# A decode step with attention and a gated FFN: later FFN weights, fp32 transposes, a PV bank shared by four pairs, and half of the last K moved to TensorE

## The chip, the cores and the metric

The kernel runs on one core of one Trainium2 chip. The metric is the device time of one execution in microseconds (us). A core has five engines that run side by side: TensorE (PE in the profile, PEld for its weight loads), VectorE (DVE), ScalarE (ACT), GpSimd (POOL) and SyncE (SP). Sixteen DMA engines bring data from memory. "Span" is the length of the profiled execution; the time that is measured from outside is about 2 us longer.

## The reference, cut to what matters

```python
# B=2, D=512, H=32 heads, Sk=8192 cached positions, Dh=128, F=1376, all bf16
q  = layernorm(x) @ wq
s  = q . k_cache * Dh**-0.5          # one query per head: a matrix-vector product
o  = softmax(s) @ v_cache
h  = x + o @ wo
g  = relu(layernorm(h) @ W_gate) * (layernorm(h) @ W_up)
out = h + g @ W_down
```

K and V are 268 MB of the 281 MB that are read, and each byte is used once.

## The kernel before

Heads go through the kernel in 32 pairs (p = 0 to 31). A pair's K is one tile of 128 partitions with 128 vectors of 128 numbers each (4 MB), and so is its V. Of the 128 columns of K, 96 are scored on VectorE, in two halves of 48: a product with q, four halving additions, a reduction. The other 32 are scored by TensorE, in four groups of eight: transpose, eviction by ACT, product with q.

```python
for p in range(NP):
    for c in range(NCH):                      # VectorE: two halves of 48 columns
        dve.wait(t_k[p])
        t_dm = prod = k_t[half c] * q         # then 4 halving additions
        t_s  = scores = reduce(prod)
        if c == 0:
            for g in range(NG):               # TensorE: 4 groups of 8 columns
                for k in range(GT):
                    i = nc.tensor.transpose(Tp[n % 2][:, k*128:(k+1)*128], k_t[:, j, :], ident[:])
                t_ev[n] = act.run(nc.scalar.activation(out=kT[n % 3][:], in_=Tp[n % 2][:], func=ACT.Copy))
                if g >= 1: score_group(p, g - 1)
            score_group(p, NG - 1)
            exp(p, 0, ...)                    # ACT, with the row sums
            if p == NP - 1: pv(p - 1)
            if p >= 1:      collect(p - 1)
        act.wait(t_s)
        exp(p, 1 + c, ...)                    # ACT works in this order
    load of K(p + 2); pv(p); load of V(p + 2) # ... cut
    # at p == 30: W_up, W_gate, then V(31) in four parts, then W_down
```

PV multiplies with the exps as weights and V as the moving operand, 512 columns wide, so four partial results stand beside each other in the bank. `collect` copies them to SBUF and adds the four diagonal blocks with four fp32 matmuls against a selection matrix, once per pair. After the last pair come the sum of the exps, PV of pair 31 column by column, the output projection, d_b (the centred input of the FFN), and the FFN.

The softmax here doesn't subtract the row's maximum and nothing guards it: scores larger than these inputs give would overflow.

## Time and profile before

| | before |
|---|---|
| time, median of 4 runs | 672.92 us (672.45 to 672.94) |
| span, instructions | 670.7 us, 8986 |
| read from memory | 281 MB |
| K of pair 30 landed | 623.98 us |
| d_b done | 662.26 us |

From the page: first line, then the slices of a fortieth of the span (share of the TensorE clock in tenths, DMA busy in tenths, GB/s) and two rows of the DMA queues (packets, MB, share of 16 engines).

```profile
span 670.7 us, 8986 instructions
PEclk9999999665565555655556656655566555565555
DMA  9999999999999999999999999999999999999994
GB/s 375 434 436 357 434 435 430 427 431 429 434 433 427 428 433 433 425 436 425 434 433 427 431 436 424 431 432 431 437 426 425 434 432 433 426 430 431 428 409 146
q1 hardware_dynamic: 15872, 281.06, 98.4%
q8 instruction: 30, 0.49, 0.3%
```

The DMA engines are busy from start to end, at about 430 GB/s. The row PEclk shows TensorE's granted clock near full for the first seven slices and at 5 to 6 tenths from then on. The first slices mean little: the trace holds no clock record before 117.8 us, and the row shows full where there is none (20 matmuls of PV take 2.31 us at 85 us and 2.31 us again at 124 us, where 0.50 is recorded). Every engine waits for the loads in mid-run, directly or in turn; the longest such row of the wait view (us in total, times, longest):

```profile
DVE prod L407 <- DMA slot<-in_A_k_cache_dram: 126.9, 30, 16.4
```

The row "q8 instruction" is easy to pass over, and I passed over it: 30 packets that carry the program itself to the engines, on the same DMA engines.

The end of the chain of work that ended last (start us, us, what):

```profile
637.07 22.22 DMA slot<-in_A_v_cache_dram
659.34 1.45 PE O L354 x48
...
662.10 0.17 DVE d_b L503
...
666.97 0.22 DVE o_c L567
```

The tail waits for the last part of V, queued behind the weights of the FFN, until 659.3. The timeline shows what else is close to the limit: VectorE's last scores, and PV of pair 30 on TensorE.

```profile
645.00 3.58 PE L361 MATMUL O<-slot,e 128*8 128x512 bf16 x32
655.05 0.55 DVE L424 TENSOR_REDUCE scores<-prod 128x48 f32<-128x384 bf16 x1
```

### The profile page before, as it was taken

The numbers are of one execution on the slowest core, as the hardware profiler recorded it, in microseconds if no ns is written. First come the engines' busy times: TensorE is split into PE (matmuls) and PEld (weight loads), VectorE is DVE, ScalarE is ACT, GpSimd is POOL, SyncE is SP. The second block draws the span as 40 slices with busy tenths as digits, with TensorE's granted clock in tenths as the row PEclk, the third lists the DMA queues.
The fourth block names the chain that finished last, engine by engine and source line by source line (L and its number), as shares of the span: only waits on it lengthen the run. The fifth ranks groups of instructions, "written<-read, shape, count | busy, mean of one in ns | idle before, by whom it ended". The sixth has DMA issues, their size and how long they took to land.

```text
span 670.7 us, 8986 instructions
## 1 busy us (share of the span) xinstructions
PE 352.0 (52%) x3868; PEld 234.1 (35%) x3868; DVE 494.4 (74%) x430; ACT 220.1 (33%) x554; POOL 2.5 (0%) x16
## 2 busy tenths in 40 slices
PE   2553355455545455554554655454556565455655
PEld 2431333233433223343322433232234443223435
DVE  1774477788768678877777887677786977678792
ACT  0631322233432234344222333322333342233340
POOL 1000000000000000000000000000000000000000
PEclk9999999665565555655556656655566555565555
DMA  9999999999999999999999999999999999999994
GB/s 375 434 436 357 434 435 430 427 431 429 434 433 427 428 433 433 425 436 425 434 433 427 431 436 424 431 432 431 437 426 425 434 432 433 426 430 431 428 409 146
DMA packets 15915, 281.63 MB, mean 420 GB/s; under 512 B 1442, under 2 KB 6916, under 8 KB 7044
## 3 DMA queue, kind: packets, MB, share of 16 engines
q1 hardware_dynamic: 15872, 281.06, 98.4%
q8 instruction: 30, 0.49, 0.3%
q14 instruction: 9, 0.07, 0.0%
q10 hardware_dynamic: 4, 0.00, 0.0%
HBM read 281.05 MB, written 0.00 MB: 419 GB/s over the span
## 4 chain that ended last, share of the span: by engine, by line
DMA 72%; DVE 22%; PE 3%; ACT 2%; issue 1%; SPq 0%; DVEq 0%
DMA slot<-in_A_k_cache_dram 68%; DVE prod L407 14%; DVE tb L415 4%; DMA slot<-in_A_v_cache_dram 3%; DVE prod L415 2%; ACT kT L440 1%; DVE scores L424 1%; PE T L434 1%; PE Ob L378 1%; ACT e L282 0%; PE S L274 0%; ACT os_sb L372 0%; PE Ob L295 0%; PE S L518 0%; PE O L560 0%
## 5 line engine op out<-in xcount | busy, mean ns | idle before, releaser
L407 DVE TENSOR_TENSOR prod<-slot,q_b 128x6144 bf16<-128x6144 bf16 x64 | 214.9, 3358 | 128.2 <-DMA slot<-in_A_k_cache_dram 126.9
L361 PE MATMUL O<-slot,e 128*8 128x512 bf16 x992 | 116.3, 621 | 143.4 <-ACT e L282 127.8
L440 ACT ACTIVATE kT<-T 128x1024 bf16<-128x1024 bf16 x128 | 126.2, 1021 | 160.2 <-PE T L434 159.4
L434 PE MATMUL T<-ident,slot 128*128 128x128 bf16 x1024 | 122.0, 305 | 65.3 <-DMA slot<-in_A_k_cache_dram 65.3
L415 DVE TENSOR_TENSOR tb<-prod 128x3072 bf16<-128x3072 bf16 (+1 forms) x128 | 148.2, 1158 | 4.4
L434 PEld LDWEIGHTS T<-ident,slot 128*128 128x128 bf16 x1024 | 99.3, 140 | 92.3 <-DMA slot<-in_A_k_cache_dram 90.6
L282 ACT ACTIVATE e<-scores 64x48 bf16<-64x48 f32 x128 | 32.8, 256 | 239.2 <-DVE scores L424 237.6
L361 PEld LDWEIGHTS O<-slot,e 128*8 128x8 bf16 x992 | 24.0, 106 | 209.6 <-ACT e L282 155.6
L415 DVE TENSOR_TENSOR prod<-tb 128x1536 bf16<-128x1536 bf16 (+1 forms) x128 | 84.2, 658 | 4.4
L378 PE MATMUL Ob<-sel,os_sb 128*128 128x2 f32 x248 | 57.5, 354 | 47.7 <-ACT os_sb L372 47.7
L378 PEld LDWEIGHTS Ob<-sel,os_sb 128*128 128x128 f32 x248 | 54.9, 327 | 51.2 <-ACT os_sb L372 51.2
L274 PE MATMUL S<-qT,kT 128*128 128x2 bf16 x1024 | 48.2, 168 | 39.2 <-ACT kT L440 38.1
L274 PEld LDWEIGHTS S<-qT,kT 128*128 128x128 bf16 x1024 | 40.7, 106 | 57.5 <-ACT kT L440 57.5
L424 DVE TENSOR_REDUCE scores<-prod 128x48 f32<-128x384 bf16 x64 | 35.4, 553 | 2.2
L282 ACT ACTIVATION_READ_ACCUMULATOR e<-scores 64x1 f32 x128 | 23.6, 185 | 0.0
L372 ACT ACTIVATE os_sb<-O 128x512 f32<-128x512 f32 x31 | 18.5, 597 | 3.4 <-PE O L361 2.7
L282 ACT ACTIVATE e<-S 64x32 bf16<-64x32 f32 x64 | 12.9, 202 | 15.0 <-PE S L274 14.2
L282 ACT ACTIVATION_READ_ACCUMULATOR e<-S 64x1 f32 x64 | 12.8, 201 | 0.7
L251 ACT ACTIVATE q_b<-O 128x512 bf16<-128x512 f32 x8 | 4.3, 595 | 15.8 <-PE O L246 15.8
L222 DVE CAST qT<-W 128x64 bf16<-128x64 f32 x1 | 0.2, 224 | 12.2 <-PE W L217 12.2
L217 PE MATMUL W<-xlT,X 128*128 128x2 bf16 x128 | 3.6, 166 | 8.8 <-DMA X<-in_A_wq_dram 8.8
L217 PEld LDWEIGHTS W<-xlT,X 128*128 128x128 bf16 x128 | 3.5, 104 | 8.8 <-DMA X<-in_A_wq_dram 8.8
(67 smaller groups left out, 58.8 us busy)
## 6 DMA issues: line engine op xcount, KB each, us to landing
slot<-in_A_k_cache_dram SPq DMA_DIRECT2D x32, 4096.0 KB, 27.7
slot<-in_A_v_cache_dram SPq DMA_DIRECT2D x31, 4096.0 KB, 31.3
X<-in_A_wq_dram SPq DMA_DIRECT2D x1, 4096.0 KB, 12.5
X<-in_A_wo_dram SPq DMA_DIRECT2D x1, 4096.0 KB, 48.7
slot<-in_A_v_cache_dram SPq DMA_DIRECT2D x1, 1536.0 KB, 19.8
slot<-in_B_W_up_dram SPq DMA_DIRECT2D x1, 1376.0 KB, 10.0
slot<-in_B_W_gate_dram SPq DMA_DIRECT2D x1, 1376.0 KB, 14.6
slot<-in_A_v_cache_dram SPq DMA_DIRECT2D x1, 1280.0 KB, 22.2
```

The costliest lines, as they stand in the source:

```text
L217: i = nc.tensor.matmul(Wp[:, h * B:(h + 1) * B], lhsT=wq[:, c, h * Dh:(h + 1) * Dh], rhs=lT[:, c * B:(c + 1) * B], start=(c == 0), stop=(c ...
L251: t_cp[m] = act.run(nc.scalar.activation(out=q_b[:, m * 512:(m + 1) * 512], in_=Op[m % 2][:], func=ACT.Copy))
L274: i = nc.tensor.matmul(Sp[p % 2][:, 2 * jj:2 * jj + 2], lhsT=kT[n % 3][:, k * 128:(k + 1) * 128], rhs=qT[:, 2 * p:2 * p + 2], start=True, ...
L282: t = act.run(nc.scalar.activation(out=e_t[p % 2][q, j0:j0 + nj, a], in_=src(q, a), func=ACT.Exp, scale=inv_sqrt_dh, accum_out=zs[q, 2 * p ...
L361: i = nc.tensor.matmul(o[g:g + 2 * VJ, :], lhsT=e_t[p % 2][:, j:j + VJ, :].rearrange("p j a -> p (j a)"), rhs=v_t[:, j:j + VJ, :].rearrang ...
L372: t_os[p] = act.run(nc.scalar.activation(out=os_sb[:], in_=Op[p % 2][:], func=ACT.Copy))
L378: i = nc.tensor.matmul(Ob[:, 2 * p:2 * p + 2], lhsT=os_sb[:, jj * Dh:(jj + 1) * Dh], rhs=sel[:, 2 * jj:2 * jj + 2], start=(jj == 0), stop= ...
L407: t_dm = dve.run(nc.vector.tensor_tensor(out=prod[:], in0=k_t[:, c * JC:(c + 1) * JC, :], in1=qv, op=ALU.mult))
L415: dve.run(nc.vector.tensor_tensor(out=o, in0=cur[:, :, 0:half], in1=cur[:, :, half:w], op=ALU.add))
L424: t_s = dve.run(nc.vector.tensor_reduce(out=sc[:], in_=cur, axis=AX.X, op=ALU.add))
L434: i = nc.tensor.transpose(Tp[n % 2][:, k * 128:(k + 1) * 128], k_t[:, j, :], ident[:])
L440: t_ev[n] = act.run(nc.scalar.activation(out=kT[n % 3][:], in_=Tp[n % 2][:], func=ACT.Copy))
```

## The change

Four things, aimed at the tail and at the load of TensorE and ACT:

1. **Order of loads.** V of the last pair is queued right after V of pair 30, in two parts; W_up, W_gate and W_down come last, each with its own semaphore.
2. **fp32 transposes.** Two neighbouring bf16 columns of K are transposed as one fp32 word, so half as many transposes are needed; the scores then use every second column and a q that is laid out to match.
3. **Shared PV bank.** Four pairs accumulate into one bank, each in eight of 32 rows (the others are multiplied with zeros), and `collect` runs once for four pairs.
4. **Half of the last K on TensorE.** Pair 31 gives 64 columns to TensorE (eight groups) and 32 to each half on VectorE.

The diff, cut to its core:

```diff
+                def split(p):
+                    ng = 2 * NG if p == NP - 1 else NG
+                    jc = (J - ng * GT) // NCH
+                    return ng, jc, [(NCH * jc, J)] + [(c * jc, (c + 1) * jc) for c in range(NCH)]
 # transposes
-                                for k in range(GT):
-                                    j = NCH * JC + g * GT + k
-                                    i = nc.tensor.transpose(
-                                        Tp[n % 2][:, k * 128:(k + 1) * 128], k_t[:, j, :], ident[:])
+                                for k in range(GT // 2):
+                                    j = parts[0][0] + g * GT + 2 * k
+                                    i = nc.tensor.transpose(
+                                        Tp[n % 2][:, k * 128:(k + 1) * 128],
+                                        k_t[:, j:j + 2, :].rearrange("p j d -> p (j d)").bitcast(F32), ident_f[:])
 # scores
+                    kv_ = kT[n % 2][:].rearrange("p (k n r) -> p k r n", n=128, r=2)
+                        for r in range(2):
+                            i = nc.tensor.matmul(
+                                Sp[p % 2][:, 2 * jj:2 * jj + 4], lhsT=kv_[:, k, r, :],
+                                rhs=q2[:, p, r, :], start=(r == 0), stop=(r == 1))
 # PV and collect
-                                o[g:g + 2 * VJ, :], lhsT=e_t[p % 2][:, j:j + VJ, :].rearrange("p j a -> p (j a)"),
+                                Op[gr % 2][c:c + 32, :], lhsT=e_t[qd][:, j // VJ, :],
-                            if p >= 1:
-                                collect(p - 1)
+                            if p >= 1 and (p % PG == 0 or p == NP - 1):
+                                collect((p - 1) // PG)
 # loads at p == 30 (... cut)
+                        sp.wait(t_pv[p - 1])
+                        for k, (j0, j1) in enumerate(((J // 2, J), (0, J // 2))):   # V(31)
                         sp.wait(*t_kfree[p])
                         for k, w in enumerate((B_W_up, B_W_gate)):
-                        load_v(p + 1, vparts)
+                        for k, (r0, r1) in enumerate(WD_PARTS):                      # W_down in two parts
```

## The prediction

> **What bounds the kernel.** The page's slice table shows DMA at 9 tenths in 39 of 40 slices, at about 430 GB/s; 281 MB at that rate take 654 of the 670.7 us span. The Trainium skill ("DMA: Bandwidth & Descriptors", section "Where 436 GB/s comes from") gives 435 GB/s as the fabric's ceiling; the trace's plateau of 425 to 437 agrees. In mid-run every engine waits for K (wait view: VectorE 127 us, PE 65 us). A pair takes 19.4 us of DMA; VectorE needs 15.5, PE and ACT less. So what the change saves there (per pair, three quarters of the selection matmuls' 1.87 us and of os_sb's 0.6 us) is off the critical path: worth about 0. The same bytes are loaded, so only the tail can move.
>
> **The tail before** (timeline, chain of waits): the last K lands at 633.7, VectorE ends its scores at 655.6, the last V part lands at 659.3, its PV ends at 660.8, d_b at 662.3, the end is at 670.7. DMA traffic ends at about 663 (one-microsecond windows). The 8.4 us from d_b on are bound by compute, not loads.
>
> **What the change does there.**
> - V of the last pair is queued 13 us earlier, ahead of 4.1 MB of FFN weights: estimated (9.5 us at 430 GB/s before 663), it lands at 653 to 654. This wait goes.
> - VectorE's last scores: 32 columns a half, not 48: 15.5 -> about 10.5 us, done at 650, not 655.6.
> - TensorE and ACT get 8 groups, not 4. ACT can start evicting only at 640.2, behind the exps of the pair before. Two groups took 2.36 us, so they end at about 649.8 (before 645.1). Then in order: PV of pair 30 3.6 us, os_sb 0.65, selection matmuls 1.9, two sums of 0.6, first half of PV 31 1.9, o_proj 1.2, second half 1.9, scale and last o_proj 0.8, d_b 0.8: d_b at about 663.7. A serial chain on PE replaces the waits for V and VectorE.
> - fp32 transposes: half as many, each with a slower weight load. The trace's fp32 selection matmuls come every 234 ns (two passes each), bf16 transposes every 128. The Trainium skill ("TensorE: Matmul & The Clock Gate", "Terms") says transpose mode makes fp32 4x faster; no run shows it yet. My estimate: one pass, 4 per group in about 0.95 us against 1.01, so the group rate stays. If a group costs 0.5 us, the tail gains 1 us; if 1.8 us, it loses about 5.
> - FFN after d_b: unchanged 8.4 us; the last weights land at about 663, needed at 665 or later.
>
> Sum: 0 in the middle, +1.4 us in the tail, less something for a cheaper transpose: nearly no change, 673.3 us, 8 in 10 between 670.3 and 675.8. Chances: faster by over 2% 0.015, within 2% 0.96, slower by over 2% 0.025.
>
> **What would show it.** Right: slices still at 9 and 430 GB/s; the chain ends not in a V load but in PE and ACT work of the last pair; V lands before 655, waited for by nobody; d_b at 662 to 665; 528 fp32 transposes at about 240 ns each. Wrong: FFN weights on the chain's end, or d_b before 661 (a tail shorter by 2 to 3 us: transposes or PE faster than assumed).
>
> **What would make it wrong.** fp32 transposes in several passes at over 450 ns; strided score weights loading slowly; a DMA plateau other than 430 GB/s; the last FFN load, in 1 KB packets, draining so unevenly that it sets the end.

## The result, and the profile after

The changed kernel took 669.17 us (median of 4 runs: 669.11, 671.62, 668.97, 669.24), before 672.92. The ratio is 0.9954 (95% interval 0.9931 to 0.9978); ratios are the mean time of one kernel's fast runs over that of the other's of the same rounds, so not quite the ratio of the medians. It is a gain of half a per cent, and below the range that I had given (670.3 to 675.8). Note the 671.62: it matters below.

The same parts of the page, after:

```profile
span 667.3 us, 7705 instructions
DMA  9999999999999999999999999999999999999995
q1 hardware_dynamic: 15600, 281.06, 98.8%
q8 instruction: 25, 0.41, 0.3%
```

DMA is as busy as before, with the same 281.06 MB of data, but 1281 instructions fewer, fetched in 25 packets instead of 30. The end of the chain has no load left in it (some of its longer pieces):

```profile
643.72 1.03 ACT kT L465
...
648.03 1.87 PE O L375 x32
...
652.33 1.59 PE O L392 x64
...
658.02 0.17 DVE d_b L536
...
663.35 0.22 DVE o_c L602
```

That is the chain that I had forecast (evictions, PV of pair 30, selection, PV of pair 31, d_b), but d_b is done at 658.2, not at 663.7. Two things differ. First, the chain starts earlier. K of pair 30 landed at 622.61 instead of 623.98; these are VectorE's first products of that pair in the timelines, before and after (in brackets the idle time ahead of it and what ended it):

```profile
623.98 3.36 DVE L407 TENSOR_TENSOR prod<-slot,q_b 128x6144 bf16<-128x6144 bf16 x1 [3.97 <-DMA slot<-in_A_k_cache_dram]
```

```profile
622.61 3.36 DVE L433 TENSOR_TENSOR prod<-slot,q_b 128x6144 bf16<-128x6144 bf16 x1 [3.94 <-DMA slot<-in_A_k_cache_dram]
```

Second, TensorE speeds up within the chain. These are two groups of transposes and PV of pair 30 in the timeline after, then the one-microsecond windows around the change (busy time and instructions of each engine, granted TensorE clock, DMA share, GB/s):

```profile
642.59 1.09 PE L458 MATMUL T<-ident_f,slot 128*128 128x128 f32 x4
...
645.01 0.64 PE L458 MATMUL T<-ident_f,slot 128*128 128x128 f32 x4
...
647.96 1.91 PE L375 MATMUL O<-slot,e 128*32 128x512 bf16 x32
```

```profile
core 0: us, PE busy (x) PEld busy (x) DVE busy (x) ACT busy (x) POOL busy (x), PEclk, DMA share, GB/s
642.00:643.00 1.00, 1.00 (x12) 0.66 (x11) 0.93 (x3) 0.88 (x2) 0.00 (x0) 0.50 1.00 426
643.00:644.00 1.00, 1.00 (x15) 0.79 (x14) 0.93 (x3) 0.72 (x2) 0.00 (x0) 0.63 1.08 459
644.00:645.00 1.00, 0.57 (x12) 0.34 (x11) 1.00 (x1) 1.00 (x2) 0.00 (x0) 1.00 0.96 410
...
653.00:654.00 1.00, 1.00 (x45) 1.00 (x42) 0.00 (x0) 0.00 (x0) 0.00 (x0) 0.99 1.00 396
654.00:655.00 1.00, 1.00 (x36) 1.00 (x35) 0.00 (x0) 0.00 (x0) 0.00 (x0) 0.50 1.07 407
```

The granted clock rises from 0.50 to 1.00 at about 643.7 and falls back at about 654. Meanwhile a group of transposes takes 0.64 us instead of 1.09, and PV 1.91 us where the kernel before needed 3.58.

So there were two theories to test, each with rivals:

- **Fetch.** The K stream runs ahead because fewer instruction packets ride on the DMA engines. Rivals: chance in the order of packets; less traffic of the engines on the buffers.
- **Clock.** The tail is shorter than forecast because the clock rises in it. Rivals: the fp32 transposes themselves; the order of loads alone; the split of K alone.

### The profile page after: what moved, and what is told of

Its sections match the earlier page's. It is cut to its first block, busy times and chain, and to the rows that moved or that the text cites. A ratio compares the mean times of both kernels' runs of the same rounds, so it can differ in the third digit from the quotient of the medians.

```text
span 667.3 us, 7705 instructions
## 1 busy us (share of the span) xinstructions
PE 320.9 (48%) x3224; PEld 198.0 (30%) x3224; DVE 490.5 (74%) x433; ACT 211.4 (32%) x535; POOL 5.8 (1%) x17
## 3 DMA queue, kind: packets, MB, share of 16 engines
q1 hardware_dynamic: 15600, 281.06, 98.8%
## 4 chain that ended last, share of the span: by engine, by line
DMA 68%; DVE 22%; PE 5%; ACT 3%; issue 1%; SPq 0%; DVEq 0%; ACTq 0%
DMA slot<-in_A_k_cache_dram 68%; DVE prod L433 14%; DVE tb L441 5%; DVE prod L441 3%; PE T L458 2%; ACT kT L465 2%; DVE scores L448 1%; PE Ob L408 1%; PE S L294 1%; ACT e L304 1%; PE O L392 0%; ACT os_sb L402 0%; PE O L375 0%; PE S L551 0%; PE Ob L319 0%
## 5 line engine op out<-in xcount | busy, mean ns | idle before, releaser
L433 DVE TENSOR_TENSOR prod<-slot,q_b 128x6144 bf16<-128x6144 bf16 (+1 forms) x64 | 212.8, 3324 | 127.1 <-DMA slot<-in_A_k_cache_dram 124.3
L375 PE MATMUL O<-slot,e 128*32 128x512 bf16 x992 | 115.8, 619 | 209.4 <-ACT e L304 133.0
L458 PE MATMUL T<-ident_f,slot 128*128 128x128 f32 x528 | 134.7, 422 | 65.4 <-DMA slot<-in_A_k_cache_dram 65.3
L441 DVE TENSOR_TENSOR tb<-prod 128x3072 bf16<-128x3072 bf16 (+2 forms) x128 | 146.9, 1147 | 4.4
L458 PEld LDWEIGHTS T<-ident_f,slot 128*128 128x128 f32 x528 | 97.2, 217 | 91.9 <-DMA slot<-in_A_k_cache_dram 90.2
L441 DVE TENSOR_TENSOR prod<-tb 128x1536 bf16<-128x1536 bf16 (+2 forms) x128 | 83.6, 653 | 4.4
L294 PE MATMUL S<-q,kT 128*128 128x4 bf16 x1056 | 50.1, 169 | 39.2 <-ACT kT L465 39.0
L294 PEld LDWEIGHTS S<-q,kT 128*128 128x128 bf16 x1056 | 43.7, 108 | 69.2 <-ACT kT L465 67.2
L448 DVE TENSOR_REDUCE scores<-prod 128x48 f32<-128x384 bf16 (+1 forms) x64 | 35.1, 549 | 2.3
L408 PEld LDWEIGHTS Ob<-sel,os_sb 128*128 128x128 f32 x64 | 13.4, 311 | 12.7 <-ACT os_sb L402 12.7
```

The source lines that it names most:

```text
L294: i = nc.tensor.matmul(Sp[p % 2][:, 2 * jj:2 * jj + 4], lhsT=kv_[:, k, r, :], rhs=q2[:, p, r, :], start=(r == 0), stop=(r == 1))
L375: i = nc.tensor.matmul(Op[gr % 2][c:c + 32, :], lhsT=e_t[qd][:, j // VJ, :], rhs=v_t[:, j:j + VJ, :].rearrange("p j d -> p (j d)"), start= ...
L408: i = nc.tensor.matmul(Ob[:, 2 * p0:2 * p0 + 2 * PG], lhsT=os_sb[:, jj * Dh:(jj + 1) * Dh], rhs=sel[:, 2 * PG * jj:2 * PG * jj + 2 * PG], ...
L433: t_dm = dve.run(nc.vector.tensor_tensor(out=prod[:, 0:jc, :], in0=k_t[:, j0:j1, :], in1=qv, op=ALU.mult))
L441: dve.run(nc.vector.tensor_tensor(out=o, in0=cur[:, :, 0:half], in1=cur[:, :, half:w], op=ALU.add))
L448: t_s = dve.run(nc.vector.tensor_reduce(out=sc[:, 0:jc], in_=cur, axis=AX.X, op=ALU.add))
```

## The experiments

All kernels below gave the right result. "Landing" is the start of VectorE's first product of pair 30; "chain" is the time from there to the end of d_b; "rise" is where the windows show the clock going to 1.00 within the last pair.

| run | instructions | fetch packets | landing | rise | chain | span | median time |
|---|---|---|---|---|---|---|---|
| before | 8986 | 30 | 623.98 | none | 38.3 | 670.7 | 672.92 |
| order_only | 8986 | 30 | 624.01 | 648 | 37.9 | 670.3 | 672.41 |
| half_only | 9118 | 30 | 624.23 | 654 | 38.7 | 672.0 | 672.76 |
| order_half | 9118 | 30 | 624.19 | 648 | 36.9 | 670.0 | 671.57 |
| before_warm | 9012 | 30 | 623.99 | 640 | 38.4 | 671.2 | 672.99 |
| bf16_T | 8761 | 29 | 624.02 | 653 | 37.6 | 670.1 | 671.95 |
| more_instr | 8965 | 30 | 624.14 | none | 39.1 | 671.8 | 672.60 |
| more_instr_55 | 11005 | 38 | 625.43 | none | 39.1 | 672.8 | 673.37 |
| changed kernel | 7705 | 25 | 622.61 | 643.7 | 35.6 | 667.3 | 669.17 |
| after_again | 7705 | 25 | 622.45 | 652 | 38.0 | 669.1 | 671.87 |
| after_third | 7705 | 25 | 622.37 | 651 | 37.7 | 668.7 | 670.59 |
| warm | 7731 | 25 | 622.68 | 635 | 35.6 | 667.3 | 668.78 |
| early | 7705 | 25 | 622.64 | 638.5 | 34.3 | 666.8 | 668.68 |
| early_again | 7705 | 25 | 622.70 | none | 34.4 | 666.5 | 668.68 |

Landing, rise, chain and span are those of the one profiled execution; the median is of all runs of that label (4 to 6). Runs of one label were on one chip.

### after_again and after_third: the changed kernel again

No edit.

> The changed kernel once more, for its spread. Theory clock (the tail is 2 us shorter because TensorE's granted clock rose from 0.5 to 1.0 within the last pair): two groups of times, about 669.1 with that rise and about 671.6 without it, and in a profile without it the PV of pair 30 takes 3.6 us, not 1.9. Theory fetch (the K stream runs 1.4 us ahead because the kernel has 1281 instructions fewer, so fewer instruction fetches ride on the DMA engines): K of pair 30 lands at 622.6 again. Rival chance: it lands anywhere between 622.6 and 624.0.

> The changed kernel on the same chip as the next run. Theory clock: again two groups of times, about 669.1 where TensorE's clock rises among the transposes of the last pair and 671.6 to 672.0 where it does not, with little in between; the profile shows which it was.

Measured: 670.91, 671.82, 671.98, 671.87, 671.97 in the first and 670.28 to 670.86 in the second, where before took 672.93 and 672.62 (ratios 0.9981 and 0.9968). So the half per cent of the first result was luck, three fast executions of four: the changed kernel's times spread over 668.97 to 671.98. Two groups with little between was too simple; there is a third at 670.3 to 670.9. The profiles explain these: the clock does rise, but late, at 652 and 651. This is PV of pair 30 and the windows around the rise in after_again:

```profile
648.54 3.60 PE L375 MATMUL O<-slot,e 128*32 128x512 bf16 x32
```

```profile
651.00:652.00 1.00, 1.00 (x12) 0.16 (x4) 0.00 (x0) 0.00 (x0) 0.00 (x0) 0.50 1.06 435
652.00:653.00 1.00, 0.30 (x6) 0.16 (x2) 0.00 (x0) 0.78 (x3) 0.00 (x0) 0.99 0.96 392
```

PV takes 3.60 us again, and only the selection after it is fast. In all fourteen profiles, every recorded stretch of one clock that ends before the run does lasts a whole number of steps of 3.41 us, and the steps lie differently against the kernel in each execution. In after_again the step from 648.62 to 652.03 lies wholly within PV, and the clock rises at its end. That is not yet the rule: in the step from 641.79 to 645.20 of the same profile PE is busy throughout with transposes and scores, as it is from 640.33 to 643.74 in the first profile, and here the clock stays at 0.50. The landing was 622.4 in both, as in the first profile, so the first gain stays and the second varies. The executions at 671.6 to 672.0 were not among the profiled ones; that they had no rise at all is inferred from more_instr below, not seen (its span without a rise is 671.8; less the 1.7 us of its later landing that is 670.1, the span of three of those executions within 0.1).

### more_instr and more_instr_55: the instructions put back

```diff
                         pv(p)
+                        for _ in range(21):        # 55 in more_instr_55
+                            i = nc.tensor.matmul(
+                                Sp[p % 2][:, 256:258], lhsT=ident[:], rhs=qT[:, 0:2], start=True, stop=True)
+                        pe.run(i)
```

> The changed kernel with 21 tiny matmuls (two columns) after each PV in the middle, about 1220 PE instructions with their weight loads, in time when PE waits for K; about as many instructions as the kernel before. Theory fetch: K of pair 30 lands at about 624.0 instead of 622.6 and the time rises by about 1.4 us, to 670.5. Rivals chance and less traffic of the engines on the buffers: landing 622.6 and time 669.1, as without them.

> The dose of the first test raised: 55 tiny matmuls after each of 30 PVs instead of 21, 3300 more PE instructions than the changed kernel, so about 13 more instruction-fetch packets (38 against 25). Theory fetch: the landing of K of pair 30 has so far followed that count (25 packets: 622.5 to 622.7; 29 or 30: 624.0 to 624.2), 0.3 us a packet, so it lands at 625.8 to 627 and the time is 673.5 to 676. Rival (anything else of the transposes or of PV, or chance): 622.5 to 624.2, and the time stays at 669 to 673.

The pages' rows of instruction packets, more_instr first, then more_instr_55:

```profile
q8 instruction: 30, 0.49, 0.3%
```

```profile
q8 instruction: 38, 0.62, 0.4%
```

The added matmuls and the next transposes in the timelines, in the same order:

```profile
622.12 0.72 PE L490 MATMUL S<-qT,ident 128*128 128x2 bf16 x21
624.16 1.97 PE L458 MATMUL T<-ident_f,slot 128*128 128x128 f32 x8 [1.33 <-DMA slot<-in_A_k_cache_dram]
```

```profile
623.64 1.62 PE L490 MATMUL S<-qT,ident 128*128 128x2 bf16 x55
625.45 1.97 PE L458 MATMUL T<-ident_f,slot 128*128 128x128 f32 x8 [0.18 <-DMA slot<-in_A_k_cache_dram]
```

The added matmuls take 0.72 and 1.62 us in PE's idle time, and PE is done with them before the K lands. With 30 packets K lands at 624.14, with 38 at 625.43 (a little short of the 625.8 to 627 that I expected). The times fit less well, since the clock of the tail moves them too: 672.60 us for more_instr, where I expected 670.5 (the changed kernel took 671.87 on that chip), and 673.37 for more_instr_55, just under the 673.5 to 676 expected. Over all fourteen profiles the landing follows the count alone: 622.37 to 622.70 with 25 packets, 623.98 to 624.23 with 29 or 30, 625.43 with 38. The transposes, PV and the order of loads differ within these groups and change nothing. Chance is out. That the added instructions cause the later landing is shown; that each packet holds up the DMA engine that carries it, and with it the K tile that waits for all sixteen, is how I read it. It fits the steps from one K landing to the next: in the profiles before, after and of more_instr, once the start is over, every step without an instruction packet (rows q8 and q14 of the DMA view) is 19.41 to 19.44 us, and the steps of 20.5 to 20.8 lie only among those with one. Here is one such step in the kernel before, and then the instruction rows of the DMA view for the window of that step, 211.83 to 232.31:

```profile
211.83 3.36 DVE L407 TENSOR_TENSOR prod<-slot,q_b 128x6144 bf16<-128x6144 bf16 x1 [1.20 <-DMA slot<-in_A_k_cache_dram]
232.31 3.36 DVE L407 TENSOR_TENSOR prod<-slot,q_b 128x6144 bf16<-128x6144 bf16 x1 [5.01 <-DMA slot<-in_A_k_cache_dram]
251.72 3.36 DVE L407 TENSOR_TENSOR prod<-slot,q_b 128x6144 bf16<-128x6144 bf16 x1 [3.94 <-DMA slot<-in_A_k_cache_dram]
```

```profile
q8 instruction: 1, 0.02, 0.3%
q14 instruction: 1, 0.01, 0.1%
```

The first step is 20.48 us, the second 19.41. Most steps with a packet are also 19.4. Which packets matter, the traces show: up to 211.83, where this late step begins, the DMA view has 8 packets in q8, so the step holds the 9th. Over all fourteen profiles 36 steps are late by 0.9 us or more, and each holds the 9th, the 17th, the 25th or the 33rd packet of q8 (in early the 9th spreads over two steps, of 20.19 and 19.92). So the landing moves by about 1.4 us for every eighth packet, and not by 0.3 us for each: before K of pair 30 lands there are two such packets in a kernel with 25, three with 29 or 30, and four with 38. Traffic of the engines on the buffers would not put the late steps at just these packets. Why it is every eighth stays open; the trace does not say which engine carries a packet. The Trainium skill ("DMA: Bandwidth & Descriptors", section "Queues, rings and completion order") says that a DMA engine takes turns between the queues that it has work for, one packet at a time; the late steps, by 0.9 to 1.6 us each, fit that but do not prove it.

### bf16_T: the plain transposes back

```diff
-                                for k in range(GT // 2):
-                                    ... two columns as one fp32 word, ident_f
+                                for k in range(GT):
+                                    j = parts[0][0] + g * GT + k
+                                    i = nc.tensor.transpose(
+                                        Tp[n % 2][:].bitcast(BF16)[:, k * 128:(k + 1) * 128], k_t[:, j, :], ident[:])
```

> The changed kernel with the bf16 transposes and the plain score matmuls of before. Theory fetch: about 990 PE instructions more, K of pair 30 about 1 us later. Theory clock: the tail is as in the changed kernel if the clock rises, groups of the last pair at 1.2 us as before, so 669.5 to 670.5 us. Rival for the tail (fp32 transposes themselves shorten it): the last pair's groups take over 10 us, not 8.8, although the clock rises.

Measured 671.95 us (670.33 to 672.05), 29 packets, landing 624.02. As changed, but with bf16 transposes, the chain takes 37.6 us with a rise at 653, against 38.0 with fp32 and a rise at 652. So the fp32 transposes do not shorten the tail by themselves: a group takes about as long either way (1.09 us fp32, 1.01 bf16 at the low clock). At the high clock the two were not compared, since here the clock rose only after the groups. What they buy is fewer instructions. The forecast of 669.5 to 670.5 held in one run of five, since the clock rose late.

### order_only, half_only, order_half: the parts of the tail alone

The kernel before with the loads of part 1, or with the split of part 4, or with both. For the loads the edit is the diff shown above; for the split:

```diff
+                    ng = 2 * NG if p == NP - 1 else NG          # groups on TensorE
+                    jc = (J - ng * GT) // NCH                   # columns of one VectorE half
-                vparts = ((0, 96, 128), (1, 0, 48), (2, 48, 88), (2, 88, 96))
+                vparts = ((0, 64, 128), (1, 0, 32), (2, 32, 56), (2, 56, 64))
```

> The kernel before with only the loads reordered: V of the last pair in two parts right after V of pair 30, FFN weights last. V then lands at 653 to 654 and nobody waits for it, but VectorE still ends the last scores at 655.6 and the exps end at 656.4; the sum of the exps 0.6, then PV 3.9: d_b at about 662.0 against 662.3, time 672.6, a gain of 0.3 us. If loads alone set the tail, the gain would be over 2 us.

> The kernel before with only the split of the last K: 64 columns on TensorE, 32 in each half on VectorE; loads in the old order. VectorE ends at about 650, but the last V part still lands at 659.3 behind the FFN weights: d_b at 662.3, time 672.9, no gain. If VectorE's scores alone set the tail, the gain would be over 2 us.

> The kernel before with two of the four parts: FFN weights last and half of the last K on TensorE; bf16 transposes and one PV bank a pair stay. Theory fetch: the instruction count is that of before, so K of pair 30 lands at 624.0. Theory clock: if the clock rises in the last pair, d_b comes 35.5 us after that landing as in the changed kernel and the time is about 670.6; if it does not, d_b comes at 663.7 as the prediction had it and the time is about 674.

Measured: 672.41 us alone with the loads (before 672.92; 0.9993, interval 0.9980 to 1.0005), 672.76 with the split (1.0002), 671.57 with both (0.9984, interval 0.9971 to 0.9998). Neither alone is distinguishable from before, as expected. With the loads moved, the chain goes through VectorE's scores, which still end at 655.6. With the split alone I had the time right and the reason only half: V still lands late (at about 660, by its issue and its time to landing), but the chain of that profile does not wait for it. It goes through the eight groups, PV and selection on PE, the groups and PV at the low clock, and d_b comes at 662.9 (this profile is of the slowest of the five executions, at 673.80). A new wait on PE had taken the place of the one for VectorE, as the prediction feared. With both changes the chain has neither V nor VectorE in it, and what is left is the PE chain and its clock. All three leave the landing at 624.0 to 624.2, as the fetch theory has it. Of the changed kernel's gain order_half holds about 1.4 us, with a clock that rose at 648 in the profile; one execution in five, at 673.46, lost it all. The chain took 36.9 us, between my two cases, and so did the time. On the chip where both ran the whole change was no faster than these two parts (671.87 in after_again): what the other two parts gained at the landing did not show in the median.

### warm and before_warm: a clock that is up in time

```diff
+                                if p == NP - 1 and g == 1:      # after two groups of transposes
+                                    pe.wait(t_os[6])
+                                    for _ in range(13):
+                                        i = nc.tensor.matmul(
+                                            Op[0][:, 0:512], lhsT=ident[:], rhs=q_b[:, 0:512], start=True, stop=True)
+                                    pe.run(i)
```

TensorE computes something useless, 512 columns wide, while it would wait for ACT. before_warm does the same in the kernel before (in its other PV bank).

> The changed kernel with 13 wide matmuls (512 columns, result unused) on PE between the first two transposed groups of the last K and the first scores, when PE waits 5.6 us for ACT. Theory clock: the clock is at 1.0 by 639 in every execution, the eight groups take about 8 us instead of 8.8, the slower group of times (671.6) vanishes, and the time is about 668.5. Rival: TensorE's clock has nothing to do with it and the time is 669.1 or, where the added matmuls delay the scores, more.

> The kernel before with the same 13 wide matmuls in front of the last pair's scores. If TensorE's clock only counts where TensorE's chain ends last, it gains nothing: the last V part still lands at 659.3 and VectorE's scores still end at 655.6, time 672.9. If a warm TensorE were worth 2 to 3 us by itself, 670 to 671.

With the wide matmuls the changed kernel takes 668.78 us, and the five runs lie between 668.45 and 669.18: the slow group of times is gone (ratio to before 0.9938). The groups of transposes did not get shorter (8.8 us, since the clock fell to 0.50 once more between 642.2 and 645.6); what counts is PV, at 1.91 us in the profile, and the selection. That both are fast in the other four executions too is inferred from their times. The kernel before takes 672.99 with the same matmuls, although its PV of pair 30 falls to 1.90 us:

```profile
644.42 1.90 PE L361 MATMUL O<-slot,e 128*8 128x512 bf16 x32
```

So a faster TensorE is worth nothing where the chain waits for V, and 0.4 to 3.1 us (medians of 669.17, 670.59 and 671.87 against 668.78, on other chips) where TensorE's own chain is the end. That is the clock theory, and the two runs together answer the rival that TensorE's clock has nothing to do with it. The changed kernel was not run on the chip of warm, so how much of the narrow times is owed to that chip is not shown.

### early and early_again: evictions that do not wait

ACT works in program order. In the changed kernel the evictions of the last K stand behind the exps of pair 30, which wait for VectorE until 638.1; the K and two groups of transposes are there at 634. So the exps were moved behind the fifth eviction:

```diff
+                                if p == NP - 1 and g == NG:
+                                    act.wait(t_late[0])
+                                    exp(p - 1, NCH, ...)            # exps of pair 30, second half
...
+                        if p == NP - 2 and c == NCH - 1:
+                            t_late = (t_s, sc)
+                            continue
                         act.wait(t_s)
                         exp(p, 1 + c, ...)
```

> The changed kernel with the evictions of the first five groups of the last K ahead of the two exps of the pair before on ACT's queue, so that they need not wait for VectorE's last scores of pair 30. The groups then run from 633.5 to about 643 instead of 638.8 to 647.6; VectorE's last scores at 649.3 become the limit for PV of the last pair, d_b at 653 to 654 instead of 658.2, and the FFN weights, which land at 661.3, become the end of the chain: end of the span about 666, time 668.0, a gain of about 1 us on the changed kernel. If the whole 4 us counted, 665.

> The changed kernel with the early evictions, on the same chip as the run before. Its end is set by the landing of the last FFN weights, not by TensorE, so the clock does not matter: one narrow group at 668.5 to 668.9, faster than the changed kernel's median by 0.4 to 3 us.

Measured 668.68 us in both (668.38 to 668.83 over ten runs), 0.9937 and 0.9940 of before, and on one chip with the changed kernel (after_third) 1.9 us faster than its median. In early_again the clock stayed at 0.50 from 634 on, PV took 3.60 us, and the time is the same. The chain shows why (from the profile of early_again):

```profile
635.16 26.79 DMA slot<-in_B_W_down_dram
661.95 0.14 issue
662.08 0.81 PE O L601 x20
```

Now the last part of W_down ends the chain, at 661.95, and TensorE has slack. d_b came at 657.0, later than the 653 to 654 that I had expected, because I had put the limit at VectorE's scores while PE, at the low clock, was still busy with PV and the selection; with the loads at the end it no longer matters. This version beats both kernels, and its times spread over 0.4 us, where the changed kernel's spread over 3.0.

## Why the prediction was right or wrong

**Right: the bound, and what it makes worthless.** DMA at 430 GB/s throughout, and the saved PE and ACT work in mid-run buys nothing by being shorter (PE is busy 320.9 us instead of 352.0). V of the last pair is waited for by nobody, and the chain ends in PE and ACT work of the last pair, as the prediction said. It also stayed within 2%.

**Wrong: "so only the tail can move".** This step of the argument took the stream of loads for fixed because its data bytes were the same. The program itself is loaded over the same DMA engines, and with 1281 instructions fewer K of pair 30 landed 1.4 us earlier. The page of the kernel before had the row with 30 packets; "worth about 0" for the saved instructions should have been 1.4 us: the 25th packet, one of those that make a step late, now comes after K of pair 30 has landed.

**Wrong: the term "PV of pair 30 3.6 us" and the others at the low clock.** I costed TensorE's new serial chain with durations that were all measured at the granted clock of 0.50, and did not ask whether a longer chain would raise it. In the two variants without a rise, more_instr and more_instr_55, the chain from landing to d_b took 39.1 us, against 39.7 in the sum of the prediction (663.7 less 624.0), so the sum itself was good to 0.6 us. With the rise at 643.7 it took 35.6: 3.5 us less. The Trainium skill ("TensorE: Matmul & The Clock Gate", section "Part 1: The HAM clock gate") says that about 3.4 us of sustained activity in a free-running window raises the clock and that this varies from run to run; the steps of 3.41 us and the rises at 643.7, 651 and 652 in one and the same kernel agree. But that PE is busy for one such window was not enough: of ten that transposes and scores filled without a pause, in the profiles of the changed kernel and its variants, three were followed by a rise. I had read the page and left it out.

**Smaller.** After d_b the end came 9.1 us later, not 8.4; 0.38 of this is a gap on PE that the chain calls issue, and its cause is open. fp32 transposes: one pass, 217 ns for a weight load, 1.09 us for a group, where I estimated 0.95; at the high clock 0.64.

The sum for the first profile: predicted span 663.7 + 8.4 = 672.1; less 1.4 (stream), less 0.6 (sum too long), less 3.5 (clock), plus 0.7 (after d_b) gives 667.3, which is the span that was measured. The forecast time of 673.3 had already taken off 1 us for a cheaper transpose, which did not come. For the executions with a late or no rise, at 670.28 to 671.98, the measured time lies within the range or at its edge; the stream's 1.4 us is missing there too. The first result was outside because of both.

Open: why it is every eighth fetch packet that delays a tile; why the clock rises in one execution at 643.7 and in another only at 652 under nearly the same instruction stream, beyond the free-running window that the skill names; and the gap of 0.38 us, with the other 0.3 us after d_b.

## What to carry to other kernels

In a kernel bound by DMA, count instructions as load: here about 256 of them made one fetch packet, every eighth packet held the loads up by about 1.4 us, and five packets fewer saved one such delay, whether or not the saved instructions were on anybody's critical path. When a change replaces a wait by a chain on TensorE, give two estimates, one at each clock. If the chain ends last, either keep TensorE warm with wide matmuls in a wait just before it, or reorder so that the chain has slack, which also makes the time steady. Look at all runs of a small gain, and repeat it: the first median of the changed kernel, with three lucky executions of four, was 1.4 and 2.7 us below those of the next two sets.

## What the Trainium skill lacked or had wrong

- "Runtime: NRT & Kernel Launch", section "Instruction fetch mechanics", has the fetch in blocks of 256 instructions over a DMA queue of its own, and calls the cost of crossing a block mostly hidden. It does not say that the fetches delay a kernel's loads. Here 25, 30 and 38 packets put the landing of the same tile at 622.5, 624.1 and 625.4 us, about 1.4 us for every eighth packet.
- "TensorE: Matmul & The Clock Gate", Part 4, says that the full clock does not engage for transposes. Here it rose at 643.7 after 3.8 us of transposes with short score matmuls in between. As the scores are no transposes, this does not refute it; what a mix of both counts for, no page says.
- The same page's rule against PE idle gaps is not enough: the clock fell to 0.50 at 654 while the profile shows PE busy for the whole of each microsecond around it, with matmuls of two columns.
- The same page gives no duration for fp32 transposes: 217 ns for the weight load, and 1.09 us (clock 0.50) or 0.64 us (1.00) for four of 128x128.
- The same page warns that the recorded clock can be wrong. What this shows is a missing record: in the kernel before, the same 16 transposes took 1.89 us at 24 us, where the profile shows 1.00 because no clock is recorded yet, and at 604 us, where 0.50 is recorded. Durations decide.
